# Delaying the attention product by one pair, spreading FFN pieces over six slots, and a new path for the weights, in a fused attention and maxout-FFN kernel

## The chip, the cores and the metric

The kernel runs on one NeuronCore of one Trainium2 chip. The metric is the time of one execution on the device in microseconds (us); lower is better. The engines are TensorE (PE; its weight loads are listed as PEld), VectorE (DVE), ScalarE (ACT), GpSimd (POOL) and SyncE (SP, which here only issues DMAs). The program is written in a framework that puts the instructions in order, and that order is not always the one of the source: at 216.84 us in the same trace four FFN matmuls stand between score chunks, although the source places them behind all four.

## The reference

Per batch (8 of them), 12 heads of attention over 448 positions with head size 64, softmax with an extra 1 in the denominator; the result, 448 rows of 768, goes through a maxout FFN.

```python
scores = scale * np.matmul(q, k.transpose(0, 1, 3, 2))          # 8 x 12 x 448 x 448
m = np.max(scores, axis=-1, keepdims=True)
e = np.exp(scores - m)
attn = e / (np.sum(e, axis=-1, keepdims=True) + np.exp(-m) + 1e-09)
x = np.matmul(attn, v)                                          # heads side by side: 3584 x 768
h = np.maximum(np.maximum(x @ w1, x @ w2), x @ w3)              # 768 x 768 each
out = h @ w_out
```

## The kernel before

Work is done in pairs of heads, six pairs a batch. I call the work around one pair a slot. In a slot TensorE makes transposes of q and k (`trT`), scores in four chunks (`stp`, two heads side by side, each a matmul of 64 rows, `64*112` in the traces), and the product with v (`av`, eight matmuls). ACT makes the exp of each chunk (`eT_all`), then Ln and Exp (`lnd_sb`, `rb_sb`) for the division. The FFN of the batch before is cut into ten pieces that fill TensorE's waits: six pieces of 18 matmuls `p_i` (x times w1, w2, w3) and four of 12 matmuls `op_ps` (times w_out). TensorE writes its results to PSUM, where the kernel keeps four buffers of 512 fp32 columns (`ps1`) and two of 2 x 512 for scores (`ps2`).

```python
wstage = ctx.enter_context(tc.tile_pool(name="wstage", bufs=1))
for i, w in enumerate((moe_w1, moe_w2, moe_w3, moe_w_out)):
    wst = wstage.tile([128, NDC, DFF], FP32, tag="wst")
    nc.sync.dma_start(out=wst, in_=w.rearrange("(dc p) f -> p dc f", p=128))
    wt = cpool.tile([128, NDC, DFF], MMDT, name=f"w{i}")
    nc.scalar.copy(out=wt, in_=wst)
# ... (cut)
for j in range(H // 2):                      # a pair of heads
    # ... loads, fp16 casts of q and k, transposes, copies to qT2 and kT2, v_sb (cut)
    for c in range(NCH):                     # 4 chunks of scores
        stp = ps2.tile([SC, 2, 512], FP32, tag="bank2")
        for hh in range(2):
            nc.tensor.matmul(out=stp[:, hh, 0:S],
                             lhsT=kT2[hh * D : hh * D + D, ts(c, SC)],
                             rhs=qT2[hh * D : hh * D + D, :], start=True, stop=True)
        nc.scalar.activation(out=eT_all[0:SC, parp, :, c, :], in_=stp[:, :, 0:S],
                             func=AF.Exp, scale=scale)
    if 2 * j < nsteps:                       # nsteps = 10
        emit_moe_piece(2 * j)
    for hh in range(2):
        # ... av = v_sb x eT_all, Ln, Exp(-), multiply into xT (cut)
        if hh == 1 and 2 * j + 1 < nsteps:
            emit_moe_piece(2 * j + 1)
```

The softmax here doesn't subtract the row's maximum and nothing guards it: scores larger than these inputs give would overflow.

## Time and profile before

| what | value |
|---|---|
| time, median of the first 4 runs | 491.56 us (490.29 to 496.03) |
| PE busy over the profiled span of 489.6 us | 421.7 us, 86% |
| attention of batch 0, no FFN work yet | until 64.9 us |
| first `p_i` that is followed by steady work | 78.1 us |
| steady period of a batch | 54.4 us |
| ACT waiting for scores | 121.6 us |

The view of busy time in stretches of the kernel before. The columns are the stretch, its length, busy us of each engine with the number of instructions, the granted TensorE clock as a share of full speed (time before the first clock record of a trace, here 18.5 us, counts as full), the DMA share and GB/s.

```profile
core 0: us, PE busy (x) PEld busy (x) DVE busy (x) ACT busy (x) POOL busy (x), PEclk, DMA share, GB/s
6.50:64.00 57.50, 37.29 (x166) 16.17 (x166) 22.46 (x60) 43.82 (x56) 0.00 (x0) 0.75 0.85 184
64.00:78.00 14.00, 2.42 (x6) 0.73 (x6) 1.89 (x5) 4.89 (x2) 0.00 (x0) 0.50 1.00 249
132.90:187.30 54.40, 50.85 (x301) 26.09 (x300) 33.34 (x75) 32.22 (x49) 0.00 (x0) 0.97 0.50 102
444.00:458.50 14.50, 10.71 (x64) 5.53 (x65) 4.44 (x10) 10.49 (x16) 0.00 (x0) 1.00 0.23 72
```

There are three regimes: batch 0, where ACT is the busiest; a stop of 14 us in which TensorE does six matmuls; and steady batches of 54.4 us in which TensorE is recorded busy for 50.85 us. The last line is the weak place of a steady batch: the pieces are used up by pair 4, so the last slot and the next first one lack filler.

The chain of work that ended last, kernel before (start, duration, what), shows what the stop is: a cast frees the only staging buffer, then the load of the third weight runs bare, then its cast, then the first useful FFN matmuls.

```profile
60.96 3.93 ACT w L115
64.91 9.06 DMA wst<-in_moe_w_dram
73.99 4.04 ACT w L115
78.08 2.42 PE p_i L151 x6
```

Two places of TensorE's timeline, kernel before (start, duration of the merged records, line, operation, output and inputs, count; in brackets the idle time before and what ended it). The first three lines are from a well-filled slot, the last two from a slot without filler.

```profile
415.22 0.59 PE L256 MATMUL stp<-qT,kT 64*112 64x448 f16 x4
415.74 0.93 PE L151 MATMUL p_i<-xT,w 128*128 128x448 f16 x4
416.62 0.40 PE L256 MATMUL stp<-qT,kT 64*112 64x448 f16 x2
...
452.09 0.58 PE L256 MATMUL stp<-qT,kT 64*112 64x448 f16 x4 [1.96 <-DVE kT L241]
453.50 0.40 PE L256 MATMUL stp<-qT,kT 64*112 64x448 f16 x2 [0.82 <-ACT eT_all L263]
```

In the unfilled slot the waits are plain. In the filled slot the record of one matmul overlaps the next (the scores of 415.22 us end at 415.81, after the `p_i` of 415.74 has started). Four `p_i` there take 416.62 - 415.74 = 0.88 us, although in long runs one takes 0.19 us (18 in 3.41 us), so 0.76 for four.

### The profile page before, as it was taken

The page shows a single profiled execution, that of the slowest core. Times are in us where ns is not written, and L with a number is a line of the kernel's source. Part 1 is how long each engine was busy: PE and PEld are TensorE (multiplying, and loading weights), DVE is VectorE, ACT ScalarE, POOL GpSimd, SP SyncE. Part 2 cuts the span into 40 slices and gives each one's busy share as a digit, 9 for nine tenths or more (in the row PEclk, how much of TensorE's full clock was granted, in tenths as well). Part 3 has the DMA queues.
Part 4 walks back from the last instruction along what each step waited for, and adds up shares of the span by engine and source line. Part 5 has one row for each costly group of instructions (what it writes and reads, how often), then busy time and mean ns, then how long its engine had stood idle before and what let it go on. Part 6 is the DMA issues. An engine that isn't in the chain of part 4 may idle for free.

```text
span 489.6 us, 6232 instructions
## 1 busy us (share of the span) xinstructions
PE 421.7 (86%) x2400; PEld 214.9 (44%) x2400; DVE 272.3 (56%) x594; ACT 277.2 (57%) x392; POOL 0.7 (0%) x6
## 2 busy tenths in 40 slices
PE   1876716999799979999799979998899979997896
PEld 0322202445344534445344634445344544454454
DVE  5343412575566655665566646756566647555454
ACT  3788835747655566457655476466755565655400
POOL 0000000000000000000000000000000000000000
PEclk9866755999899999999899999999899989999999
DMA  9981969946644182807553392608471410002003
GB/s 187 262 194 27 280 208 283 208 81 145 137 96 76 52 191 59 152 1 176 107 119 51 77 199 58 120 1 197 86 148 23 111 59 1 1 29 71 15 0 112
DMA packets 137053, 53.87 MB, mean 110 GB/s; under 512 B 130368, under 2 KB 130368, under 8 KB 137024
## 3 DMA queue, kind: packets, MB, share of 16 engines
q1 hardware_dynamic: 137024, 53.48, 50.9%
q8 instruction: 18, 0.29, 0.3%
q14 instruction: 11, 0.09, 0.1%
HBM read 42.47 MB, written 11.01 MB: 109 GB/s over the span
## 4 chain that ended last, share of the span: by engine, by line
PE 76%; ACT 13%; DVE 4%; DMA 4%; issue 2%; SPq 0%
PE p_i L151 32%; PE av L281 18%; PE stp L256 11%; PE op_ps L172 11%; ACT eT_all L263 6%; ACT rb_sb L291 3%; ACT w L115 2%; DVE xT L292 2%; PE trT L228 2%; PE trT L233 2%; DMA wst<-in_moe_w_dram 2%; ACT lnd_sb L289 2%; DMA k__97<-in_k_dram 2%; DVE o_sb L179 1%; DVE qT L239 1%
## 5 line engine op out<-in xcount | busy, mean ns | idle before, releaser
L263 ACT ACTIVATE eT_all<-stp 112x896 f16<-112x896 f32 x192 | 161.2, 920 | 121.9 <-PE stp L256 121.6
L151 PE MATMUL p_i<-xT,w 128*128 128x448 f16 x864 | 185.1, 357 | 17.2 <-ACT w L115 15.9
L151 PEld LDWEIGHTS <-w 128*128 128x128 f16 x864 | 79.2, 99 | 100.8 <-issue 21.1
L281 PE MATMUL av<-eT_all,v_sb 112*128 112x448 f16 (+1 forms) x384 | 106.5, 401 | 2.5 <-ACT eT_all L263 2.5
L256 PE MATMUL stp<-qT,kT 64*112 64x448 f16 x384 | 70.3, 398 | 33.7 <-DVE kT L241 17.8
L161 DVE TENSOR_TENSOR hT<-hT,p_i 128x448 f16<-128x448 f16 x96 | 59.7, 622 | 57.8 <-PE p_i L151 56.9
L172 PE MATMUL op_ps<-w,hT 128*112 128x384 f16 x384 | 75.1, 328 | 0.0
L289 ACT ACTIVATE lnd_sb<-av 64x448 f32<-64x448 f32 x96 | 48.5, 534 | 44.9 <-PE av L281 44.9
L292 DVE TENSOR_TENSOR xT<-av,rb_sb 64x448 f16<-64x448 f32 x96 | 59.2, 616 | 18.9 <-ACT rb_sb L291 15.0
L256 PEld LDWEIGHTS <-kT 64*112 64x112 f16 x384 | 26.1, 128 | 82.7 <-issue 49.1
L172 PEld LDWEIGHTS <-hT 128*112 128x112 f16 x384 | 47.4, 129 | 19.6 <-issue 6.1
L281 PEld LDWEIGHTS <-v_sb 112*128 112x128 f16 (+1 forms) x384 | 36.1, 106 | 43.0 <-issue 22.4
L291 ACT ACTIVATE rb_sb<-lnd_sb 64x448 f32<-64x448 f32 x96 | 52.0, 571 | 1.3
L179 DVE TENSOR_SCALAR o_sb<-op_ps 112x384 f32<-112x384 f32 x64 | 35.6, 556 | 21.5 <-PE op_ps L172 21.0
L159 DVE CAST hT<-p_i 128x448 f16<-128x448 f32 x48 | 29.9, 622 | 12.0 <-PE p_i L151 10.2
L228 PE MATMUL trT<-ident,q 112*128 112x112 f16 x192 | 29.6, 232 | 7.0 <-DVE q L214 6.5
L233 PE MATMUL trT<-ident,k 112*128 112x112 f16 x192 | 29.4, 233 | 3.0 <-DVE k L220 3.0
L228 PEld LDWEIGHTS <-q 112*128 112x128 f16 x192 | 20.9, 109 | 13.3 <-DVE q L214 6.5
L239 DVE COPY qT<-trT 128x448 f16<-128x448 f16 x48 | 18.5, 384 | 13.6 <-PE trT L233 13.6
L233 PEld LDWEIGHTS <-k 112*128 112x128 f16 x192 | 21.2, 111 | 10.5 <-issue 4.4
L115 ACT CAST w<-wst 128x4608 f16<-128x4608 f32 x4 | 16.2, 4043 | 9.1 <-DMA wst<-in_moe_w_dram 9.1
L241 DVE COPY kT<-trT 128x448 f16<-128x448 f16 x48 | 18.3, 381 | 0.0
(60 smaller groups left out, 74.3 us busy)
## 6 DMA issues: line engine op xcount, KB each, us to landing
out_dram<-o_sb SPq DMA_DIRECT2D x32, 336.0 KB, 2.8
wst<-in_moe_w_dram SPq DMA_DIRECT2D x3, 2304.0 KB, 9.1
wst<-in_moe_w_out_dram SPq DMA_DIRECT2D x1, 2304.0 KB, 9.3
q__95<-in_q_dram SPq DMA_DIRECT2D x1, 672.0 KB, 5.3
k__97<-in_k_dram SPq DMA_DIRECT2D x1, 672.0 KB, 8.1
v__99<-in_v_dram SPq DMA_DIRECT2D x1, 672.0 KB, 9.3
q__101<-in_q_dram SPq DMA_DIRECT2D x1, 672.0 KB, 9.5
k__103<-in_k_dram SPq DMA_DIRECT2D x1, 672.0 KB, 9.5
```

What stands on the lines that cost most here:

```text
L151: nc.tensor.matmul(out=p_i[:, 0:S], lhsT=w_sb[i][:, dc, ts(fc, 128)], rhs=xTp[:, dc, :], start=(dc == 0), stop=(dc == NDC - 1),)
L161: nc.vector.tensor_tensor(out=hTp[:, fc, :], in0=hTp[:, fc, :], in1=p_i[:, 0:S], op=ALU.max)
L172: nc.tensor.matmul(out=op_ps[0:SC, 0:NW], lhsT=hTp[:, fc, ts(t, SC)], rhs=wout_sb[:, fc, ts(nh, NW)], start=(fc == 0), stop=(fc == NFC - 1),)
L179: nc.vector.tensor_scalar(out=o_sb[:, ts(nh, NW)], in0=op_ps[0:SC, 0:NW], scalar1=1.0 / LAMBDA, scalar2=None, op0=ALU.mult,)
L228: nc.tensor.transpose(out=trT[:, 0, ts(c, SC)], in_=q16[:, c, :, :], identity=ident16[0:SC, 0:SC],)
L233: nc.tensor.transpose(out=trT[:, 1, ts(c, SC)], in_=k16[:, c, :, :], identity=ident16[0:SC, 0:SC],)
L256: nc.tensor.matmul(out=stp[:, hh, 0:S], lhsT=kT2[hh * D : hh * D + D, ts(c, SC)], rhs=qT2[hh * D : hh * D + D, :], start=True, stop=True,)
L263: nc.scalar.activation(out=eT_all[0:SC, parp, :, c, :], in_=stp[:, :, 0:S], func=AF.Exp, scale=scale,)
L281: nc.tensor.matmul(out=av[:, 0:S], lhsT=v_sb[0:kk, vslot, c, :], rhs=eT_all[0:kk, parp, hh, c, :], start=(c == 0), stop=(c == NCH - 1),)
L289: nc.scalar.activation(out=lnd_sb, in_=av[D : 2 * D, 0:S], func=AF.Ln)
L291: nc.scalar.activation(out=rb_sb, in_=lnd_sb, func=AF.Exp, scale=-1.0)
L292: nc.vector.tensor_tensor(out=xT[(h % HD2) * D : (h % HD2) * D + D, h // HD2, :], in0=av[0:D, 0:S], in1=rb_sb, op=ALU.mult,)
```

## The change

Its intent is threefold. (1) `av` and the division of a pair are issued one slot later, after the next pair's transposes, so that exp, Ln and Exp hide behind other TensorE work. (2) The ten FFN pieces are spread over all six slots instead of the first five. (3) The weights get two staging buffers, casts on GpSimd instead of ScalarE, and the last two loads go through GpSimd's DMA queue. The memset of `ones_f32` also shrinks to the 1792 columns that are used; in the trace before it ended at 5.12 us, ahead of the first cast of q at 6.02, which waited 0.62 us for its DMA.

```diff
-    ones_f32 = cpool.tile([128, 4096], FP32, name="ones_f32")
+    ones_f32 = cpool.tile([128, 1792], FP32, name="ones_f32")
-    wstage = ctx.enter_context(tc.tile_pool(name="wstage", bufs=1))
+    wstage = ctx.enter_context(tc.tile_pool(name="wstage", bufs=2))
-        nc.sync.dma_start(out=wst, in_=...)
+        (nc.sync if i < 2 else nc.gpsimd).dma_start(out=wst, in_=...)
-        nc.scalar.copy(out=wt, in_=wst)
+        nc.gpsimd.tensor_copy(out=wt, in_=wst)
 # ... the loop, cut to its core:
-    for b in range(B + 1):
-        for j in range(H // 2):
-            # casts, transposes, scores + exp of pair j, piece 2j,
-            # av + division of pair j, piece 2j+1
+    for it in range(len(pairs) + 1):
+        # casts, transposes of pair `it`
+        if prev is not None:
+            # av + division of pair `it - 1`
+                if hh == 1 and pj not in (1, 2):
+                    moe_next()
+            if pj == H // 2 - 1:
+                # what is left of the old FFN; this batch's FFN becomes the pending one
+        if not flush:
+            # scores + exp of pair `it`
+            moe_next()
+            prev = (b, j, parp)
```

More of the change, by code (lines that the diff above doesn't have):

```diff
@@ L112 @@
         wst = wstage.tile([128, NDC, DFF], FP32, tag="wst")
-        nc.sync.dma_start(out=wst, in_=w.rearrange("(dc p) f -> p dc f", p=128))
+        (nc.sync if i < 2 else nc.gpsimd).dma_start(out=wst, in_=w.rearrange("(dc p) f -> p dc f", p=128))
         wt = cpool.tile([128, NDC, DFF], MMDT, name=f"w{i}")
-        nc.scalar.copy(out=wt, in_=wst)
+        nc.gpsimd.tensor_copy(out=wt, in_=wst)
         w_sb.append(wt)
@@ L189, with moe_next @@
     nsteps = NFC + NCH
-    for b in range(B + 1):
-        if b == B:
-            for s_ in range(nsteps):
-                emit_moe_piece(s_)
-            break
-        xT = xt_pool.tile([128, NDC, S], MMDT, tag="xT")
-        hT = ht_pool.tile([128, NFC, S], MMDT, tag="hT")
-        for j in range(H // 2):
+    pairs = [(bb, jj) for bb in range(B) for jj in range(H // 2)]
+    cur = {}
+    prev = None
+    moe_state = [0]
+    def moe_next():
+        if pending[0] is not None and moe_state[0] < nsteps:
+            emit_moe_piece(moe_state[0])
+            moe_state[0] += 1
+    for it in range(len(pairs) + 1):
+        flush = it == len(pairs)
+        if not flush:
+            b, j = pairs[it]
             hb = (2 * j) // HB
             jb = j - hb * (HB // 2)
-            parp = j % PPAR
+            parp = it % PPAR
+            if j == 0:
+                xT_b = xt_pool.tile([128, NDC, S], MMDT, tag="xT")
+                hT_b = ht_pool.tile([128, NFC, S], MMDT, tag="hT")
+                cur[b] = (xT_b, hT_b)
             if jb == 0:
@@ L204 @@
                     blocks[(b, hb)] = load_block(b, hb)
-                q12, k12, v12 = blocks[(b, hb)]
-                idx = blk_order.index((b, hb))
-                if idx + 1 < len(blk_order):
-                    nxt = blk_order[idx + 1]
+                bidx = blk_order.index((b, hb))
+                if bidx + 1 < len(blk_order):
+                    nxt = blk_order[bidx + 1]
                     if nxt not in blocks:
                         blocks[nxt] = load_block(*nxt)
+            q12, k12, v12 = blocks[(b, hb)]
             q16 = p16_pool.tile([SC, NCH, 2, D], MMDT, tag="q16")
@@ L251 @@
                 )
+        if prev is not None:
+            pb, pj, parq = prev
+            xTp_, hTp_ = cur[pb]
+            for hh in range(2):
+                h = 2 * pj + hh
+                ih = pb * H + h
+                vslot = ih % VB
+                av = ps1.tile([128, 512], FP32, tag="bank1")
+                for c in range(NCH):
+                    kk = SC + 1 if c == NCH - 1 else SC
+                    nc.tensor.matmul(
+                        out=av[:, 0:S],
+                        lhsT=v_sb[0:kk, vslot, c, :],
+                        rhs=eT_all[0:kk, parq, hh, c, :],
+                        start=(c == 0),
+                        stop=(c == NCH - 1),
+                    )
+                lnd_sb = small.tile([D, S], FP32, tag="lnd_sb")
+                nc.scalar.activation(out=lnd_sb, in_=av[D : 2 * D, 0:S], func=AF.Ln)
+                rb_sb = small.tile([D, S], FP32, tag="rb_sb")
+                nc.scalar.activation(out=rb_sb, in_=lnd_sb, func=AF.Exp, scale=-1.0)
+                nc.vector.tensor_tensor(
+                    out=xTp_[(h % HD2) * D : (h % HD2) * D + D, h // HD2, :],
+                    in0=av[0:D, 0:S],
+                    in1=rb_sb,
+                    op=ALU.mult,
+                )
+                if hh == 1 and pj not in (1, 2):
+                    moe_next()
+            if pj == H // 2 - 1:
+                while pending[0] is not None and moe_state[0] < nsteps:
+                    emit_moe_piece(moe_state[0])
+                    moe_state[0] += 1
+                pending[0] = (pb, xTp_, hTp_)
+                moe_state[0] = 0
+            prev = None
+        if not flush:
             for c in range(NCH):
@@ L268 @@
                 )
-            if 2 * j < nsteps:
-                emit_moe_piece(2 * j)
-            for hh in range(2):
-                h = 2 * j + hh
-                ih = b * H + h
-                vslot = ih % VB
-                av = ps1.tile([128, 512], FP32, tag="bank1")
-                for c in range(NCH):
-                    kk = SC + 1 if c == NCH - 1 else SC
-                    nc.tensor.matmul(
-                        out=av[:, 0:S],
-                        lhsT=v_sb[0:kk, vslot, c, :],
-                        rhs=eT_all[0:kk, parp, hh, c, :],
-                        start=(c == 0),
-                        stop=(c == NCH - 1),
-                    )
-                lnd_sb = small.tile([D, S], FP32, tag="lnd_sb")
-                nc.scalar.activation(out=lnd_sb, in_=av[D : 2 * D, 0:S], func=AF.Ln)
-                rb_sb = small.tile([D, S], FP32, tag="rb_sb")
-                nc.scalar.activation(out=rb_sb, in_=lnd_sb, func=AF.Exp, scale=-1.0)
-                nc.vector.tensor_tensor(
-                    out=xT[(h % HD2) * D : (h % HD2) * D + D, h // HD2, :],
-                    in0=av[0:D, 0:S],
-                    in1=rb_sb,
-                    op=ALU.mult,
-                )
-                if hh == 1 and 2 * j + 1 < nsteps:
-                    emit_moe_piece(2 * j + 1)
-        for s_ in range(H, nsteps):
-            emit_moe_piece(s_)
-        pending[0] = (b, xT, hT)
+            moe_next()
+            prev = (b, j, parp)
+    while moe_state[0] < nsteps:
+        emit_moe_piece(moe_state[0])
+        moe_state[0] += 1
 _INS = ['q', 'k', 'v', 'moe_w1', 'moe_w2', 'moe_w3', 'moe_w_out']
```

## The prediction

> **What bounds it now.** Read from the stretch table, the chain of waits and the PE timeline:
>
> 1. Batch 0, 0 to 64.9 us: attention alone. ACT is the limit (43.8 us busy in the 57.5 us from 6.5): scores, exp, av, Ln/Exp in series, about 7 us a pair, plus two 4 us weight casts.
> 2. 64.9 to 78.1 us: all stops for a weight. With one staging buffer a load waits for the last cast: 9.06 us load and 4.04 us cast stand bare in the chain.
> 3. Seven steady batches, about 54.3 us apart. PE is nearly gapless for most of one (403.3 to 441.5: 38.17 us busy), but the ten FFN pieces end with pair 4, so pair 5 and the next pair 0 have too little filler: from 444 to 458.5 PE is busy 10.7 of 14.5 us; one batch earlier (398 to 403.3) the granted clock is 0.76. The tail from 458.5 is 31 us of FFN and the last store.
>
> **What the change does.** It delays av of a pair by one iteration (softmax chain hidden), spreads ten pieces over all six slots, doubles the weight staging, moves the casts to POOL and the last two weight loads to POOL's queue. The matmuls are the same, and so is the tail: 108 p_i and 48 op_ps.
>
> **Steady batch (start-to-start times of the PE timeline):** 108 p_i x 0.19 + 48 av x 0.19 + six pairs of scores (0.52+0.33+0.33) + 48 op_ps x 0.165 + six transposes of 0.4 = 20.5+9.1+7.1+7.9+2.4 = 47.0 us. ACT needs 32.2 us a batch, DVE 33.5: both fit. In the two one-piece slots PE needs 6.5 us and ACT's loop (four exps 3.7, Ln/Exp 2.1, handovers) about 6.3: small leaks. I take 48 us, 6.3 less than now, times seven: 44 us.
>
> **Start.** Pair cadence in batch 0 about 6.4 us (ACT 5.8 plus handovers at half clock): p_i begins near 52 to 56 us. Weights: DMA moves q/k/v at 215 GB/s and weights at about 410 GB/s (slices of the DMA view), so w1 and w2 land near 27 and 33 us. A POOL cast of 4608 columns is not in this trace[...]. So p_i starts near 54 instead of 78: 24 us saved.
>
> Sum: 54 + 7 x 48 + 32 + 2 outside the span = 424 us. Range 412 to 440.
>
> [...]
>
> **Right if:** steady period 47 to 49 us, PE busy over 95% and clock 0.99 or more there; first p_i before 58 us; no 9 us load in the chain; ACT waits for stp shrink from 122 us. **Wrong if:** POOL casts take over 10 us or block DVE, so that w3 comes after 65 us; the first k/q block behind the weights arrives late; bank rotation (four buffers) or DVE order stops PE in the one-piece slots; the period stays above 50 us.
>
> Chances: faster by over 2% 0.97, within 2% 0.02, slower 0.01.

The sum, 54 + 7 x 48 + 32 + 2, came to 424 us.

## The result, and the profile after

The changed kernel took 440.99 us in the median of 11 runs (438.86 to 449.42), against 493.85 us for the kernel before in the runs beside it. The ratio is 0.8939, 95% interval 0.8909 to 0.8969. All ratios in this text are computed in one way from the fast runs of one kernel and of the kernel before in the same rounds; they are not quite the ratio of the medians, which include slow runs. The result lies 17 us above the predicted 424 and just above the upper end of the range, 440.

The stretches of the changed kernel, with the same columns:

```profile
6.50:54.20 47.70, 34.17 (x145) 12.77 (x146) 25.12 (x50) 31.53 (x46) 13.81 (x5) 0.77 1.18 275
54.20:106.64 52.44, 51.70 (x313) 26.39 (x311) 38.98 (x89) 33.71 (x51) 4.16 (x1) 0.98 0.89 181
156.60:206.60 50.00, 49.37 (x303) 25.62 (x301) 33.11 (x75) 32.54 (x49) 0.00 (x0) 1.00 0.57 111
```

The start went as predicted, with the first `p_i` at 54.2 us. In the chain of waits the bare load is gone, and `av` of the last pair leads straight into the FFN:

```profile
51.42 2.99 PE av L272 x8
54.41 2.57 PE p_i L151 x8
```

The steady period fell from 54.4 to 50.0 us. Of these 4.4 us, 1.5 are busy time (50.85 against 49.37 us, at a granted clock of 0.97 against 1.00), the rest is idle time.

But the steady batch did not go as predicted: it took 50.0 us instead of 48, although TensorE is recorded busy for 49.37 us of it (98.7%) and the clock is 1.00. Every sign that the prediction had named as right, except the period itself, came true: busy time over 95%, full clock, first `p_i` before 58 us, no bare load. ACT's wait for scores also shrank (list of waits; the columns are engine and line, waited for, us in total, times, longest). In the kernel before:

```profile
ACT eT_all L263 <- PE stp L256: 121.6, 43, 4.1
```

The same list of the changed kernel:

```profile
ACT eT_all L310 <- PE stp L303: 59.1, 33, 7.2
```

So the 2 us a batch are lost inside a TensorE that looks full. TensorE's timeline of the changed kernel, two neighbouring slots; the first has a piece after `av` as well (cut off), the second has only one piece:

```profile
216.84 0.93 PE L151 MATMUL p_i<-xT_b,w 128*128 128x448 f16 x4
217.73 0.40 PE L303 MATMUL stp<-qT,kT 64*112 64x448 f16 x2
218.06 0.55 PE L151 MATMUL p_i<-xT_b,w 128*128 128x448 f16 x2
...
221.54 1.68 PE L272 MATMUL av<-eT_all,v_sb 112*128 112x448 f16 x8
223.16 0.58 PE L303 MATMUL stp<-qT,kT 64*112 64x448 f16 x4
223.68 1.12 PE L151 MATMUL p_i<-xT_b,w 128*128 128x448 f16 x5
225.07 0.40 PE L303 MATMUL stp<-qT,kT 64*112 64x448 f16 x2 [0.28 <-ACT eT_all L310]
225.40 0.93 PE L151 MATMUL p_i<-xT_b,w 128*128 128x448 f16 x4
```

ACT's timeline for the second of these slots:

```profile
223.56 0.53 ACT L280 ACTIVATE lnd_sb<-av 64x448 f32<-64x448 f32 x1
224.11 0.92 ACT L310 ACTIVATE eT_all<-stp 112x896 f16<-112x896 f32 x1
```

Two losses can be read here. In the one-piece slot, scores of chunk 2 start at 225.07, right when the exp of chunk 0 ends (224.11 + 0.92 = 225.03) and frees a score buffer; five `p_i` (0.95 us) are too little filler in between. In both slots, filler followed by scores takes longer than its matmuls: four `p_i` 217.73 - 216.84 = 0.89 instead of 0.76. Two theories fit the latter. Theory A: it is the same wait for exp. Theory B: it is a cost of TensorE for going from 128-row to 64-row matmuls. They differ in what more filler will do, and the experiments test that.

### The profile page after: what moved, and what is told of

The parts are those of the page before. It is cut to its first block, busy times and chain, and to the rows that moved or that the text cites. A ratio compares the mean times of both kernels' runs of the same rounds, so it can differ in the third digit from the quotient of the medians.

```text
span 438.5 us, 6224 instructions
## 1 busy us (share of the span) xinstructions
PE 409.5 (93%) x2400; PEld 209.0 (48%) x2400; DVE 276.0 (63%) x594; ACT 264.6 (60%) x388; POOL 18.7 (4%) x12
## 4 chain that ended last, share of the span: by engine, by line
PE 83%; ACT 8%; issue 3%; DVE 2%; DMA 2%; SPq 0%
PE p_i L151 36%; PE op_ps L172 16%; PE av L272 15%; PE stp L303 12%; ACT eT_all L310 4%; ACT lnd_sb L280 2%; PE trT L242 2%; ACT rb_sb L282 2%; PE trT L237 2%; DMA k__97<-in_k_dram 2%; DVE k L229 1%; DVE xT_b L283 0%; DVE qT L248 0%; DVE kT L250 0%; DVE q L223 0%
## 5 line engine op out<-in xcount | busy, mean ns | idle before, releaser
L151 PE MATMUL p_i<-xT_b,w 128*128 128x448 f16 x864 | 181.7, 355 | 0.0
L272 PE MATMUL av<-eT_all,v_sb 112*128 112x448 f16 (+1 forms) x384 | 89.9, 373 | 2.6 <-DVE xT_b L283 1.4
L161 DVE TENSOR_TENSOR hT_b<-hT_b,p_i 128x448 f16<-128x448 f16 x96 | 59.6, 621 | 45.2 <-PE p_i L151 44.8
L283 DVE TENSOR_TENSOR xT_b<-av,rb_sb 64x448 f16<-64x448 f32 x96 | 59.2, 617 | 35.3 <-ACT rb_sb L282 32.1
L172 PE MATMUL op_ps<-w,hT_b 128*112 128x384 f16 x384 | 73.7, 331 | 0.0
L172 PEld LDWEIGHTS <-hT_b 128*112 128x112 f16 x384 | 46.3, 129 | 21.7 <-issue 10.3
L159 DVE CAST hT_b<-p_i 128x448 f16<-128x448 f32 x48 | 30.0, 624 | 22.7 <-PE p_i L151 20.8
L237 PE MATMUL trT<-ident,q 112*128 112x112 f16 x192 | 26.5, 219 | 7.5 <-DVE q L223 7.3
L242 PE MATMUL trT<-ident,k 112*128 112x112 f16 x192 | 25.3, 217 | 4.7 <-DVE k L229 4.7
L115 POOL CAST w<-wst 128x4608 f16<-128x4608 f32 x4 | 16.2, 4060 | 47.7 <-DMA wst<-in_moe_w_dram 36.2
```

The costliest lines, as they stand in the source:

```text
L151: nc.tensor.matmul(out=p_i[:, 0:S], lhsT=w_sb[i][:, dc, ts(fc, 128)], rhs=xTp[:, dc, :], start=(dc == 0), stop=(dc == NDC - 1),)
L161: nc.vector.tensor_tensor(out=hTp[:, fc, :], in0=hTp[:, fc, :], in1=p_i[:, 0:S], op=ALU.max)
L172: nc.tensor.matmul(out=op_ps[0:SC, 0:NW], lhsT=hTp[:, fc, ts(t, SC)], rhs=wout_sb[:, fc, ts(nh, NW)], start=(fc == 0), stop=(fc == NFC - 1),)
L237: nc.tensor.transpose(out=trT[:, 0, ts(c, SC)], in_=q16[:, c, :, :], identity=ident16[0:SC, 0:SC],)
L242: nc.tensor.transpose(out=trT[:, 1, ts(c, SC)], in_=k16[:, c, :, :], identity=ident16[0:SC, 0:SC],)
L272: nc.tensor.matmul(out=av[:, 0:S], lhsT=v_sb[0:kk, vslot, c, :], rhs=eT_all[0:kk, parq, hh, c, :], start=(c == 0), stop=(c == NCH - 1),)
```

## The experiments

All twelve runs gave correct results; y1_after_again repeats the source of the change, and z1_two_two_again that of y3_two_two. They were made on three chips, with four executions of each kernel; medians are of all executions. Slow executions (1 of 11 of the change, 1 of 4 of x3_fine, 2 of 4 each of y1, y3 and z1) are left out of the ratios but not of the medians, so compare ratios. The steady period is the distance between the same instruction in neighbouring batches of the trace. The first `p_i` needs only the first two heads of its batch, so it is a rough mark of the start.

| run | median us | ratio to before (95%) | first `p_i` us | steady period us |
|---|---|---|---|---|
| before | 491.8 to 493.9 | 1 | 78.1 (after the stop) | 54.4 |
| the change | 440.99 | 0.8939 (0.8909 to 0.8969) | 54.2 | 50.0 |
| x1_loop_only | 459.89 | 0.9359 (0.9309 to 0.9409) | 78.0 (after the stop) | 50.0 |
| x2_weights_only | 482.30 | 0.9797 (0.9732 to 0.9863) | 64.6 | 54.4 |
| z4_spread_only | 464.99 | 0.9432 (0.9402 to 0.9462) | 79.7 (after the stop) | 50.2 |
| y2_no_spread | 442.23 | 0.8980 (0.8925 to 0.9034) | 52.1 | 50.1 |
| y1_after_again | 445.04 | 0.8942 (0.8890 to 0.8994) | 58.2 | 50.0 |
| x3_fine | 433.32 | 0.8815 (0.8767 to 0.8862) | 52.5 | 48.8 |
| y4_fine_padded | 433.25 | 0.8801 (0.8768 to 0.8834) | 53.7 | 48.8 |
| y3_two_two | 427.51 | 0.8617 (0.8568 to 0.8666) | 56.5 | 47.3 |
| z1_two_two_again | 424.17 | 0.8535 (0.8493 to 0.8577) | 50.3 | 47.3 |
| z2_two_two_chunks | 420.47 | 0.8550 (0.8507 to 0.8593) | 51.3 | 47.3 |
| x4_cast_chunks | 437.77 | 0.8930 (0.8863 to 0.8996) | 49.8 | 50.0 |
| z3_casts_act | 451.31 | 0.9153 (0.9121 to 0.9185) | 56.5 | 50.0 |

In the changed loop the period is the same to 0.1 us from the second FFN batch to the sixth, and for the same source it is the same in another trace (49.98 us in the change and y1, 47.32 in y3 and z1). What scatters between executions is the start and the first FFN batch: y1's slow execution reached the second FFN batch at 114.2 us, the change at 106.6, and from there both took 331.9 us. The profiled executions of y1_after_again and y3_two_two were slow.

### The parts of the change, one at a time

**x1_loop_only**: the new loop with the old weight path.

```diff
-        (nc.sync if i < 2 else nc.gpsimd).dma_start(out=wst, in_=...)
+        nc.sync.dma_start(out=wst, in_=...)
-        nc.gpsimd.tensor_copy(out=wt, in_=wst)
+        nc.scalar.copy(out=wt, in_=wst)
 # and one staging buffer, ones_f32 of 4096 columns, as before
```

> The new loop with the old weight path (one staging buffer, all loads on the sync queue, casts on ScalarE). If the gains of the two halves add up, this keeps the steady period of 50 us and gives back the start: first FFN matmul near 74 to 80 us instead of 54, total 441 + 22 = 463 us, 458 to 470. If the new loop hides the late weights behind attention work of the next batch, it lands nearer 450.

Measured: 459.89 us, inside the range of the additive theory. The period is 50.0 us, and the stop for the weights is back.

**x2_weights_only**: the old loop with the new weight path (the same edit the other way round).

> The old loop with the new weight path. Additive theory: first FFN matmul near 56 us instead of 78, steady period unchanged at 54.3 us, total about 470 us (462 to 476). If the casts on GpSimd block VectorE enough to matter, the first FFN matmul comes later than 62 us and the total stays above 478.

Measured: 482.30 us. The ratio, 0.9797, is below 1, but whether the gain reaches 2% is open (interval 0.9732 to 0.9863). The time is above the range of the additive theory and above 478, the bound that I had named for blocking by GpSimd; the first `p_i`, at 64.6 us, is also later than 62. The weights were ready in time (the third cast ended at 47.55 us), but the attention of batch 0 was not: its last `av` ended at 61.5 us, against 56.0 in the kernel before, which has the same loop. The chain of waits of x2_weights_only shows VectorE instructions held up beside GpSimd's first two casts (a third, of 4.0 us, stands beside the third cast):

```profile
28.27 3.88 DVE k L220
34.49 3.78 DVE v_sb L245
```

So the cause named, blocking, is in the chain; the longest VectorE instruction in the chain of the kernel before up to 65 us takes 0.44 us. The saving at the start is 78.1 - 64.6 = 13.5 us, not 22. Its parts are not additive: loop alone saves about 32 us of 492, weights alone about 10, both together 53 of 494. The early weights pay in full only when attention of batch 0 keeps up with them. The second buffer and the GpSimd queue were not tested apart.

**y2_no_spread**: the change with two pieces a slot again; and **z4_spread_only**: the kernel before with the spread alone.

```diff
 # y2_no_spread
-                if hh == 1 and pj not in (1, 2):
+                if hh == 1:
 # z4_spread_only, in the loop of before
-            if 2 * j < nsteps:
-                emit_moe_piece(2 * j)
+            moe_next()
-                if hh == 1 and 2 * j + 1 < nsteps:
-                    emit_moe_piece(2 * j + 1)
+                if hh == 1 and j not in (1, 2):
+                    moe_next()
```

> The changed kernel, only the spreading of the pieces undone: two pieces a slot from the first on, so that the slot of pair 0 has almost no filler. If the spread matters as the change intends, that slot runs at the speed of the exp chain (about 6 us for 3.1 us of TensorE work), [...]and the period rises from 50 to about 52 us: total 452 us (447 to 458). If the delay of av alone does the work, the total stays within 3 us of the yardstick.

> The kernel before, only the ten FFN pieces spread over the six slots as in the change (av not delayed, old weights). In the old loop a slot with too little filler lasts about 8 us; two of them with one p_i piece each instead of one with none: period 54.4 to about 52.5 us, total about 480 us (473 to 485). If spreading is worth nothing here either, the period stays at 54.4 us and the total at 491.

The first expectation failed for y2_no_spread, and its alternative (within 3 us of the yardstick) held: the fast runs average 442.2 us against 440.3 of y1_after_again. z4_spread_only gained more than its range. One steady batch of y2_no_spread in the view of stretches:

```profile
152.80:202.90 50.10, 49.61 (x301) 25.55 (x300) 33.02 (x74) 32.68 (x49) 0.00 (x0) 1.00 0.57 111
```

And one of z4_spread_only, in the same view:

```profile
182.30:232.56 50.26, 49.73 (x301) 25.23 (x300) 33.48 (x75) 32.32 (x48) 0.00 (x0) 1.00 0.52 111
```

Undoing the spread leaves the period at 50.1 us and the total unchanged within the intervals (0.8980 against 0.8942). The spread alone, without any delay of `av`, brings the old loop from 54.4 to 50.2 us. So in the steady state each of the two is enough, and the second adds nothing: both do away with the same unfilled stretch. What the delay brings beyond that shows in batch 0, where there is no filler to spread, and only beside the new weight path. With it the last `av` of batch 0 ends at 54.4 us in the change (50 to 58.4 in the other traces of a delayed loop with casts on GpSimd) and at 61.5 in x2_weights_only. With the old path it ends at 56.2 in x1_loop_only and 56.0 in the kernel before: no gain. The chain of the change holds one blocked VectorE instruction there, that of x2_weights_only three. So the delay seems to help batch 0 to bear the blocking; but this is read from single traces whose clocks in batch 0 differ, and no run tests it.

**z3_casts_act**: the change with only the casts put back on ScalarE.

```diff
-        nc.gpsimd.tensor_copy(out=wt, in_=wst)
+        nc.scalar.copy(out=wt, in_=wst)
```

> The changed kernel with only the casts put back on ScalarE (two staging buffers and the GpSimd queue loads stay). If moving the casts off ScalarE is what frees the start, three casts of 4 us stand in the limiting queue of batch 0, less the blocking of VectorE that goes (about 4 us): first FFN matmul near 60 us, total 445 to 450 us. If the second buffer is what counts and the blocking costs as much as the casts, 437 to 443 us.

Measured: 451.31 us, a little above the first range. The move to GpSimd is worth about 2% here (0.9153 against 0.8939, of two different calls). In this trace the third load is issued only at 46.36 us, since it waits for the first cast, which the scheduler placed late in ACT's queue. The first `p_i`, at 56.5 us, comes before the 60 that I expected, but it misleads here: the last `av` of batch 0 ends at 64.8 us, against 54.4 in the change. ScalarE had the third cast ahead of the batch's last exp; it waited 3.74 us for the load and then cast for 4.03 us, and that exp and the last `av` came behind it. These are 7.8 of the 10.4 us; the rest was not separated.

### The steady batch

**x3_fine**: the FFN in groups of six matmuls, each group placed between score chunks, four or five a slot.

```diff
-            moe_next()                       # one piece of 18 or 12 matmuls behind the scores
+                if c > 0:                    # inside the loop over the 4 score chunks
+                    moe_groups(PLAN[j][c])   # 6 matmuls after chunks 1, 2 and 3
 # ... (cut: the change-over to the next batch's FFN moves behind chunk 1 of pair 0)
 # and after av: moe_groups(PLAN[(pj + 1) % 6][0]);  PLAN rows: (2,1,1,1) or (1,1,1,1)
```

> The changed kernel with the FFN work handed out in groups of six matmuls, so that a whole group (1.14 us) stands between the scores of chunks 1 and 2, 2 and 3, and after 3, and 4 or 5 groups in each of the six slots. Same matmuls. Theory A (PE in order waits for the exp that frees one of two score buffers, and the filler stands behind that wait): the waits go, period falls from 50.0 to 47.0 to 47.6 us, total 441 - 7 x 2.6 = 422 us (418 to 427). Theory B (switching between 64-row score matmuls and 128-row matmuls costs PE about 0.1 us each time, whatever ScalarE does): the number of switches is the same or higher, the period stays at 49.5 us or more, total 437 to 443 us.

Measured: 433.32 us and a period of 48.8 us, between the two theories. Neither alone is right. TensorE's timeline of x3_fine:

```profile
217.08 0.59 PE L314 MATMUL stp<-qT,kT 64*112 64x448 f16 x4
217.60 1.31 PE L153 MATMUL p_i<-xT_b,w 128*128 128x448 f16 x6
218.84 0.40 PE L314 MATMUL stp<-qT,kT 64*112 64x448 f16 x2
219.17 1.31 PE L153 MATMUL p_i<-xT_b,w 128*128 128x448 f16 x6
```

The weight loads of x3_fine in the same stretch, from its timeline:

```profile
218.84 0.13 PEld L314 LDWEIGHTS <-kT 64*112 64x112 f16 x2 [0.37 <-issue]
219.16 0.11 PEld L153 LDWEIGHTS <-w 128*128 128x128 f16 x2 [0.20 <-issue]
```

No wait for exp is left in these slots (three exps run back to back from 217.52 in 2.67 us, so that of chunk 0 ended near 218.4, before the scores of chunk 2 at 218.84, and that of chunk 1 near 219.3, before those of chunk 3 at 220.40), yet six `p_i` take 218.84 - 217.60 = 1.24 us instead of 1.14. The weight loads suggest why: kT's load starts at 218.84, together with the first score matmul, not ahead of it; and the first `p_i` behind the scores, at 219.17, has its load at 219.16, again bare. So the longer filler removed 50.0 - 48.8 = 1.2 us a batch, which is Theory A's part, and 18 switches of 0.10 us, 1.8 us a batch, remain. The trace of the change agrees: in one steady batch (156.6 to 206.6 us) all twelve groups of scores in the middle of a slot start 0.05 us after an exp ends, and beyond the 0.10 us each their filler runs over by 1.3 us in sum. The brackets show only two of these waits, of 0.28 us each.

**y4_fine_padded**: x3_fine with k padded by zeros, so that scores use all 128 rows. The result is the same; the two heads of a chunk no longer run side by side.

```diff
+    kT_pad = cpool.tile([128, 4, 2, S], MMDT, name="kT_pad")   # zeroed once on GpSimd
-            nc.vector.tensor_copy(out=kT2, in_=trT[:, 1, :])
+            for hh in range(2):
+                nc.vector.tensor_copy(out=kT_pad[hh * D : hh * D + D, it % 4, hh, :],
+                                      in_=trT[hh * D : hh * D + D, 1, :])
-                        lhsT=kT2[hh * D : hh * D + D, ts(c, SC)],
-                        rhs=qT2[hh * D : hh * D + D, :],
+                        lhsT=kT_pad[:, it % 4, hh, ts(c, SC)],
+                        rhs=qT2,
```

> The fine-group kernel with k padded by zeros so that every score matmul uses all 128 rows (the same result, no 64-row matmuls; the two heads of a chunk no longer run side by side). Theory B': the bare weight loads go, a group of six p_i ahead of scores takes 1.14 instead of 1.24 us start to start, while a chunk's scores cost 2 x 0.19 instead of 0.26 to 0.33 us; the two nearly cancel, period 48.6 to 49.3 us, total 431 to 437 us. If the 1.24 us has another cause, it stays at 1.24 and the period rises to about 51 us, total 445 us or more.

Measured: 433.25 us, period 48.8 us, as the weight-load theory expects. TensorE's timeline of y4_fine_padded:

```profile
210.66 1.30 PE L156 MATMUL p_i<-xT_b,w 128*128 128x448 f16 x6
211.79 0.54 PE L320 MATMUL stp<-qT,kT_pad 128*112 128x448 f16 x2
212.17 0.35 PE L156 MATMUL p_i<-xT_b,w 128*128 128x448 f16 x1
```

The weight loads of y4_fine_padded in the same stretch:

```profile
211.60 0.32 PEld L320 LDWEIGHTS <-kT_pad 128*112 128x112 f16 x2
211.98 0.29 PEld L156 LDWEIGHTS <-w 128*128 128x128 f16 x2
```

Six `p_i` now take 211.79 - 210.66 = 1.13 us, and two scores 0.38, exactly 0.19 each. Both loads start 0.19 us before their matmul, during the matmul ahead (211.60 against 211.79, 211.98 against 212.17). The switch cost is thus tied to the 64-row matmuls. That the late weight load itself is the cost, and not something else in the change from 128 to 64 rows, fits the traces but was not tested apart. The cost happens to be as large as what running two heads side by side saves: the period is 48.8 us in both.

**y3_two_two** and, as a yardstick on another chip, **z1_two_two_again**: x3_fine with two groups after chunk 1, none after chunk 2, so that there are two switches into the scores a slot instead of three.

```diff
-    PLAN rows (2, 1, 1, 1) or (1, 1, 1, 1)
+    PLAN rows (2, 2, 0, 1) or (1, 2, 0, 1)   # in pair 0 the two after chunk 1 are one old, one new
```

> The fine-group kernel with the scores of a pair issued as two plus two chunks instead of two, one, one: two switches into the scores a slot instead of three. Theory B' (each change between 64-row score matmuls and 128-row matmuls lays a weight load bare, about 0.10 us into the scores and 0.14 us behind each group of scores): a slot with four p_i groups falls from 7.95 to 7.71 us, the period from 48.8 to 47.4 us, total about 423 us (420 to 427). If the rest of the loss were waits for exp, the longer distance to the second half would cost, not gain: 432 us or more.

> The fine-group kernel with two plus two score chunks once more, as the yardstick of this call: steady period 47.3 us, total 423 to 429 us.

Measured: 427.51 and 424.17 us, ratios 0.8617 and 0.8535; the period is 47.3 us in both, where 47.4 had been worked out. The total of y3 is 0.5 us above its range (two of its four runs were slow). TensorE's timeline of z1_two_two_again, part of one slot:

```profile
216.09 1.30 PE L153 MATMUL p_i<-xT_b,w 128*128 128x448 f16 x6
217.32 0.59 PE L314 MATMUL stp<-qT,kT 64*112 64x448 f16 x4
217.83 2.44 PE L153 MATMUL p_i<-xT_b,w 128*128 128x448 f16 x12
```

The same instruction in z1_two_two_again two batches apart, which gives the period, (241.66 - 147.02) / 2 = 47.3:

```profile
147.02 0.59 PE L314 MATMUL stp<-qT,kT 64*112 64x448 f16 x4
...
241.66 0.59 PE L314 MATMUL stp<-qT,kT 64*112 64x448 f16 x4
```

Four scores in one run take 0.51 us, where two runs of two take 0.66, and one switch of 0.10 us a slot is saved. This is the version that beats both kernels: the same matmuls as the change, 0.85 to 0.86 of the time before.

### The start

In the changed kernel a cast on VectorE that takes 0.42 us elsewhere took up to 3.829 us. The view of one source line by tile, changed kernel (count, then shortest, median and longest in ns, first and last start):

```profile
L229 DVE CAST k<-k__103 x3: 415/418/3829, 23.1 to 33.8; 112x512 f16<-112x512 f32 x3
```

VectorE's timeline of the changed kernel there:

```profile
30.02 4.16 DVE L229 CAST k<-k__103 112x512 f16<-112x512 f32 x2
```

GpSimd's timeline of the changed kernel at the same time:

```profile
29.54 4.03 POOL L115 CAST w<-wst 128x4608 f16<-128x4608 f32 x1 [28.24 <-DMA wst<-in_moe_w_dram]
```

The first of the two casts ends near 33.8, just after GpSimd's cast ends at 33.57. So beside the GpSimd cast a VectorE cast was held off here (3.829 us against 0.42), but not every instruction: a copy of kT out of PSUM at 29.72 us, beside the same cast, took its usual 0.38 us. The blocked cast stands in the chain of waits of the change:

```profile
30.10 3.76 DVE k L229
```

**x4_cast_chunks** cuts each GpSimd cast into six, and **z2_two_two_chunks** does the same to the two-plus-two kernel. **y1_after_again** was to be the yardstick.

```diff
-        nc.gpsimd.tensor_copy(out=wt, in_=wst)
+        for dc in range(NDC):
+            nc.gpsimd.tensor_copy(out=wt[:, dc, :], in_=wst[:, dc, :])
```

> The changed kernel with each weight cast on GpSimd cut into six instructions of 768 columns. Theory L (a GpSimd cast holds off VectorE casts and copies for its whole 4 us, which delays the attention of batch 0): the long VectorE casts (2 to 4 us) shrink below 1 us, the first FFN matmul comes at 50 to 52 us instead of 54, total 437 to 439 us. Rival (the start is set by ScalarE and by the third weight, not by the blocking): first FFN matmul stays at 53.5 to 55 us, total 440 to 442 us.

> The yardstick plus the weight casts on GpSimd cut into six. If blocking of VectorE behind 4 us casts delays the start, the first FFN matmul comes 2 to 5 us earlier and the total is 1 to 4 us under the yardstick; the period stays at 47.3 us. If the six short casts block as much in sum, the totals agree within 1.5 us.

> The changed kernel once more, as the yardstick for the others of this call on the same chip: 439 to 443 us, steady period 50.0 us.

Measured: x4 437.77 us with the first `p_i` at 49.8 us, on the side of the blocking theory; but its ratio, 0.8930, is that of the change itself (0.8939), within an interval of 0.007 to either side. The granted clock differs too (0.84 in x4 from 36 to 54 us, 0.50 in the change), so one trace of each doesn't isolate the start. z2's ratio, 0.8550, agrees with its yardstick's 0.8535, and its first `p_i` is not earlier (51.3 against 50.3). As a gain in time this is inconclusive, and the sign that the long VectorE instructions would shrink below 1 us failed. The trace of x4 also shows that cutting does not always let VectorE in: one v_sb copy (0.29 us elsewhere) waits through nearly all of a run of six short casts on GpSimd. VectorE's timeline of x4_cast_chunks:

```profile
35.25 4.23 DVE L255 TENSOR_SCALAR v_sb<-v__105 112x256 f16<-112x256 f32 x1
```

GpSimd's timeline of x4_cast_chunks:

```profile
34.66 4.67 POOL L116 CAST w<-wst 128x768 f16<-128x768 f32 x6
```

y1_after_again had two fast runs (439.04 and 441.58 us) and two slow ones (448.5 and 449.26), so its median is above what I expected. The view gives its slow profiled execution a granted clock of 0.996, but that figure is of no use: this trace has no clock record before 60.7 us, and the view counts such time as full. The matmuls tell otherwise: the last eight `av` of batch 0 take 58.21 - 55.22 = 2.99 us, 0.37 each, twice the 0.19 at full clock, and those before them are as slow from 15 us on. So TensorE ran at half speed through batch 0 there, where the trace of the change has 13.7 us at full clock (the other delayed loops with casts on GpSimd 7 to 24). A low clock is therefore a candidate for the slow start. Blocking is another: which VectorE instruction is long beside a GpSimd cast differs between the traces (beside the second cast it is a v_sb copy of 2.89 us at 37.20 in the change, and a run of two of them in y1, 4.32 us from 35.60). In y1's first FFN batch, 3.5 us longer than the change's, a v_sb copy of 2.08 us beside GpSimd's fourth cast held up `av` by 1.89 us, and the clock was 0.50 for 3.4 us after it, which by estimate costs 1.7. Neither was isolated; what makes the slow runs is not shown.

## Why the prediction was wrong

The predicted sum was 54 + 7 x 48 + 32 + 2 = 424 us. The trace gives 54.2 (first `p_i`), 52.4 for the first batch, then five of 49.98 and one of 48.98, and 33.0 for the tail, 438.5 us of span, and 2.5 us outside it.

- **The start, 54 us: right (54.2), partly by luck.** On the path of the weights a GpSimd cast took 4.03 us, where the forecast had an estimate that no trace showed; the first load landed at 29.5, not 27, and the third weight was ready at 50.8. That path did not set the start: the chain before the first `p_i` is all attention of batch 0, for which the prediction had 52 to 56, with one blocked VectorE cast of 3.76 us in it. The prediction named such blocking among the ways to be wrong; it had no term for it in its sum. The same source started at 58.2 us in y1's slow execution.
- **The tail, 32 us: right (33.0).**
- **The steady period, 48 us: wrong (50.0).** This is the step that failed, and it is a mis-sized term. "108 p_i x 0.19 + 48 av x 0.19 + ... = 47.0 us" took start-to-start times from long uninterrupted runs and applied them to filler that is cut into runs of four, two and six. Each run of filler that ends at 64-row scores costs 0.10 us more (y4_fine_padded removes exactly this), 18 times a batch, 1.8 us. The "small leaks" of 1 us, the waits for exp, were about right: x3_fine removed 1.2 us. 47.0 + 1.8 + 1.2 = 50.0. Over six steady periods this is the better part of the miss: 9.9 us in the five whole ones, 1.0 in the last.
- **The first batch, 48 us: 52.4.** The trace accounts for most of these 4.4 us. 2.0 are the same loss as in a steady batch. 1.0 is work that only moved: this stretch holds four scores and eight transposes more than a steady one, and the last, of 48.98 us, as many less. The granted clock was still 0.50 until 56.4 us, which by estimate from that share costs 1.1 us. No run tested this apart.
- **Why the change helps: partly right.** The weights had to come earlier, and the unfilled stretch had to go. But I counted delay and spread as one remedy; y2_no_spread and z4_spread_only show that for the steady state either of them is enough, and the traces suggest that the delay earns its keep in batch 0, beside GpSimd's casts.
- **The signs to look for were too weak.** PE busy above 95% and a full clock were both fulfilled (98.7%, 1.00) while 2.7 us a batch could still be gained (47.3 in y3_two_two).

## What to carry to other kernels

When TensorE looks full (98.7% busy here), measure start to start over whole alternating patterns, not the spacing inside long runs, and count the switches from full-row to partial-row matmuls (0.10 us each here, 18 a batch). Check a granted-clock figure against the spacing of the matmuls too; y1_after_again's could not be trusted. Put enough filler between two users of a small set of buffers that the buffer is free when the second comes, and group the partial-row matmuls: here the first took 1.2 us off a batch (50.0 to 48.8) and the second 1.5 (48.8 to 47.3). Before adding two remedies for one gap, test each alone: the second may do nothing there, and its worth, if any, may lie elsewhere.
